# Six of the sequence DFT's passes, not five, as seven block products, with the sums of x and the weight chunks at earlier steps

## The chip, the cores and the metric

The kernel runs on one core of one Trainium2 chip. The metric is device time in microseconds (us) of one execution. The profile's names: PE is TensorE's matmul, PEld its weight load, DVE is VectorE, ACT is ScalarE, POOL is GpSimd, SP is SyncE, which here issues the transfers, and SPq is SP's queue.

## The reference, cut to what matters

One sublayer mixes along both axes by Fourier matrices, a second one is a gated feed-forward layer. x is 2048 x 448, the inner width is 1792, all in float32:

```
h  = x + Cr @ (ln(x) @ Dr.T) - Ci @ (ln(x) @ Di.T)     # Cr, Ci: 2048 x 2048
out = h + (gelu(ln(h) @ w_gate) * (ln(h) @ w_up)) @ w_down
```

The change lies in the first line: the products with the two 2048 x 2048 matrices. The kernel multiplies them with ln(x) first and applies the 448-wide matrices afterwards.

## The kernel before, in words

Every float32 operand is split in two halves of 16 bits, a high part (made on ACT) and the remainder (made on DVE), and each product is three matmuls: high by high, high by low, low by high.

The sequence DFT runs in `N_STEPS` = 64 steps (L405), written out in program order; nothing reorders them later. Steps 0 to 15 go over the 16 row tiles of x. From step 16 on, four steps make a pass, and each pass gives 256 rows of the result, for the real or the imaginary matrix. A step needs 128 x 1024 numbers of the matrix, called unit n: `seq_load` brings them in as `wr` (two transfers on SP, some steps ahead), `seq_hi` on ACT and `seq_lo` on DVE make the tile `ws`. Those two run three steps ahead of the matmuls that read the tile. There are 6 buffers of the tag `ws` and 5 of `wr`.

An ordinary step (L637) is 8 block products of three matmuls, 24 in all, each over 448 columns. A step from `FAST` on (L441) uses Strassen's scheme in one level: two groups of 7 block products over half the columns, that is 42 matmuls over 224 columns (`fast_mm`, L509). For this, DVE forms sums of blocks of the matrix (`fast_sums`, L460 to L462, tile `sums`), which ACT and DVE split (`fast_raw`, `fast_split`) into two `ws` tiles per unit, named `ws44_0` and `ws44_1` for unit 44. A unit is then made two steps ahead, except the first three, whose places are the list `fast_at` (L796). At the end of a fast pass `fast_out` puts the seven sums together on DVE (L538, tile `e`) and splits them into `zs`. After an ordinary pass ACT and DVE split the accumulators into `zs` directly (`z_out`).

The Strassen products also need sums of blocks of ln(x), the eight pieces t0 to t7: `t_load` brings rows of x in again, `t_norm` normalizes them on ACT, `t_sums` (DVE, L571 to L574) forms the sums, `t_hi` and `t_lo` split them. Step n of a pass reads pieces 2(n mod 4) and 2(n mod 4) + 1. A piece's steps stand in a table at L789.

Once two passes for the same rows are done, `z_turn` has SP transpose `zs` into `z` by four DMAs, and `hid_mm` (L719) applies the 448-wide matrix, 21 matmuls for each of two halves; these are put in at fixed steps: 36 and 37, 44 and 45, 52 and 53, 60 and 61 among others. Between all this the same engines prepare the feed-forward layer: 9 chunks of the gate and up weights (`Weights`, table `DFT_F` at L737) are loaded, summed on DVE in step n, split in steps n + 1 and n + 2, and stored to DRAM after step n + 3. Their raw tiles have two buffers, so a chunk's load waits until the chunk before the last has been split.

SP is one queue in program order: what stands behind a transfer that waits for DVE or PE waits too. The accumulators of the passes lie in a ring of seven PSUM banks; the seven banks are given names again for the feed-forward layer at L1289, where chunk 0 takes `a0`, `a1`, `a2` and chunk 1 takes `X`, `Y`, `Z`.

Of the kernel before, what the change touches and what calls it, by code (L numbers as in the profile page):

```python
# [32 lines left out]
def kernel(  # L33
# [172 lines left out]
    def down_load(n):  # L206
        place = (fpool, "dn_w", 3) if n > 1 else (fops, "xn" if n % 2 else "tt", 1)
        wd32[n] = place[0].tile([P, 4, HD], F32, tag=place[1], bufs=place[2], name=f"wd32_{n}")
        nc.sync.dma_start(wd32[n].rearrange("p (k c) d -> p k (c d)", k=2), w_down[n])
# [148 lines left out]
    def x_load(i):  # L358
        xt[i] = dft.tile([P, 1, D], F32, tag="xt", bufs=3, name=f"x{i}")
        nc.sync.dma_start(xt[i][:, 0, :], x[i * P : (i + 1) * P, :])  # L360
# [44 lines left out]
    N_STEPS = NT + 8 * (NP - 2)  # L405
# [7 lines left out]
    def seq_load(n):  # L413
        wr[n] = dft.tile([P, 8 * P], F32, tag="wr", bufs=5, name=f"wr{n}")
        if n < NT:
            nc.sync.dma_start(wr[n].rearrange("p (b t) -> p b t", b=4), w_seq[8 * (n % 2) + n // 2])
            return
        p, part, qq = step_of(n)
        for i in range(2):
            dst = wr[n][:, i * 4 * P : (i + 1) * 4 * P].rearrange("p (g t) -> p g t", g=2)  # L420
            nc.sync.dma_start(dst, w_seq[8 * p + 2 * qq + i][:, 2 * part : 2 * part + 2, :])
# [4 lines left out]
    def seq_hi(n):  # L426
        ws_tile(n)
        hi_part(ws[n][:, 0], wr[n], D_SC)

    def seq_lo(n):  # L430
        lo_part(ws[n][:, 1], wr[n], ws[n][:, 0], D_SC)
# [6 lines left out]

    FAST = N_STEPS - 20  # L441
    A_RAW = ("A12", "A11", "A22")
    FORMS = ("S3", "S1", "S2", "S4")
    T_OPS = ("T1", "T3", "T4", "T2")
# [22 lines left out]
    def fast_places(n):  # L467
        ring = dict(tag="ws", bufs=6)
        return (dict(tag="raw", bufs=2, pool=prep), ring) if n == FAST + 2 else (ring, ring)

# [27 lines left out]
    def fast_begin(n):  # L498
        fast_acc[n] = [ps_seq.tile([P, 512], F32, tag="mm", name=f"acc_f{n}_{k}") for k in range(4)]
# [59 lines left out]
    def t_load(j):  # L559
        tx[j] = [dft.tile([P, 1, D], F32, tag="xt", bufs=3, name=f"tx{j}_{k}")[:, 0, :] for k in range(2)]  # L560
        for k in range(2):
            i = 2 * j + 1 - k
            nc.sync.dma_start(tx[j][k], x[i * P : (i + 1) * P, :])

    def t_norm(j):
        for k in range(2):
            x_affine(tx[j][k], tx[j][k], 2 * j + 1 - k)

    def t_sums(j):
        (o1, o2), (e1, e2) = [(t[:, 0:HD], t[:, HD:D]) for t in tx[j]]  # L570
        V.tensor_sub(o1, o2, o1)  # L571
        V.tensor_sub(o2, e2, o2)
        V.tensor_sub(e2, e2, o1)
        V.tensor_sub(e1, e1, e2)  # L574
# [19 lines left out]
    def t_hi(j):  # L594
        fast_t[j] = t_tile(j)
        for dst, src in zip(t_views(j, 0), tx[j]):
            hi_part(dst, src)

    def t_lo(j):
        for dst, src, hi in zip(t_views(j, 1), tx[j], t_views(j, 0)):  # L600
            lo_part(dst, src, hi)
# [27 lines left out]
    def seq_acc(p, part, g, last=False):  # L629
        pool, tag = (ps_tr, "tr") if last else (ps_seq, "mm")  # L630
        acc[p, part, g] = pool.tile([P, 512], F32, tag=tag, name=f"acc{p}_{part}{g}")
# [102 lines left out]


    gu, gw = {}, {}
    DFT_F = ((13, 17), (11, 20), (9, 22), (7, 25), (5, 27), (3, 30), (0, 32), (1, 35), (2, 37))  # L737
    JIT_F = range(4, 13, 2)

    early, after = {}, {}  # L740

    def at(where, n, *what):
        where.setdefault(n, []).extend(what)
# [7 lines left out]
        nc.sync.dma_start(gw[f], w_dram[f])  # L751

    for i, (f, n) in enumerate(DFT_F):
        at(after, (n - 4, 0), lambda f=f, k=i % 2: gu.update({f: Weights(f, k)}))
        at(early, n, lambda f=f: gu[f].sums())
        at(early, n + 1, lambda f=f: gu[f].split(True))
        at(early, n + 2, lambda f=f: gu[f].split(False))
        at(after, (n + 3, 0), lambda f=f: gu[f].store())
# [6 lines left out]
    for p, (n, half) in enumerate(turns):  # L765
        b, j = divmod(p, 2)
# [19 lines left out]
    at(early, N_STEPS - 2, lambda: h_tile(NB - 1, 1))  # L786
    at(early, N_STEPS - 1, gelu_table)
    at(after, (N_STEPS - 2, 0), lambda: down_load(0), lambda: down_load(1))
    for j, n in ((0, 17), (1, 20), (4, 24), (5, 29), (6, 36), (2, 39), (3, 42), (7, 45)):  # L789
        at(after, (n - 2, 1), lambda j=j: t_load(j))  # L790
        at(early, n, lambda j=j: t_norm(j), lambda j=j: t_sums(j))
        at(after, (n, 0), lambda j=j: t_hi(j))
        at(after, (n, 1), lambda j=j: t_lo(j))


    fast_at = [FAST + n for n in (-4, -2, -1)] + list(range(FAST + 1, N_STEPS - 2))  # L796

# [34 lines left out]
    for n in range(N_STEPS):  # L832
        if n == 0:
            for key in first:
                seq_acc(*key, last=key == first[-1])
        elif n >= FAST and n % 4 == 0:
            fast_begin(n)
# [3 lines left out]
        if n + 3 < NT:  # L841
            x_load(n + 3)
        if n + 3 < FAST:
            seq_load(n + 5)

        if 0 < n < FAST - 3:
            seq_hi(n + 3)
# [6 lines left out]
        if n == 0:  # L854
            seq_lo(2)
        if n + 3 < FAST:
            seq_lo(n + 3)
# [406 lines left out]
    for q, t0, step, when in ((2, 6, 3, AT_A), (3, 14, 6, AT_B)):  # L1264
# [22 lines left out]
    right.close()  # L1287
    ps_ff = {
        tag: ctx.enter_context(tc.tile_pool(name=f"ps_{tag}", bufs=1, space=bass.MemoryType.PSUM, reuse_waits="tile"))  # L1289
        for tag in ("a0", "a1", "a3", "X", "Y", "Z", "a2")  # L1290
    }
    ps_ff["tr"] = ps_tr

# [11 lines left out]
    for t in range(NF):  # L1305
        w = gu.get(t + 2) if t + 2 in JIT_F else None
        n = PREP_AT.get(t)
# [90 lines left out]
    for t in range(NF, N_GU):  # L1398
        now, ahead = steps[t], steps.get(t + 1, [])
# [59 lines left out]
        for p, t0 in ended.items():  # L1459
            each = 3 if p < 3 else 2  # L1460
            n = each * (t - t0)
# [106 lines left out]
```

## Time and profile before

| | |
|---|---|
| median of 3 runs | 705.34 us (705.0 to 705.86) |
| the profiled execution, its own time | 706.23 us |
| its span, first to last instruction | 704.5 us |
| PE busy | 699.3 us |
| DVE busy | 536.5 us |
| ACT busy | 394.7 us |
| granted clock of TensorE | 1.0 throughout |

The span is 1.73 us shorter than the profiled execution's time, and that execution is 0.89 us above the median. In a row of a group, "x24" is the number of instructions, then come busy time and the mean of one; matmuls overlap each other, so their mean is longer than the distance between two. In the timeline and the chain of waits the first number is the start in us, the second the length. In the windows, each engine has its busy time in the stretch. In brackets stands the idle time ahead of a row and what ended it.

### The profile page before, as it was taken

Reading aid. Unit: us, or ns where it says so; the run is one execution under the profiler, and the core shown is the slowest. Engines: PE = TensorE matmul, PEld = TensorE weight load, DVE = VectorE, ACT = ScalarE, POOL = GpSimd, SP = SyncE. Lnnn points to the kernel's source line nnn. Section 1 sums busy time; section 2 is a strip of 40 time slices with the busy share of each in tenths; the row PEclk is TensorE's granted clock in tenths of the full one; section 3 lists DMA queues with packets and bytes.
Section 4 is the critical chain, followed back from the end, with each engine's and each line's share of the span. In section 5 each row is a group of like instructions: output and inputs, shape, how many; then the busy total and the mean of one; then the engine's idle time right before and its main releaser. Section 6 shows DMA issues by size and latency. Waiting matters only on the chain.

```text
span 704.5 us, 13462 instructions
## 1 busy us (share of the span) xinstructions
PE 699.3 (99%) x5092; PEld 494.0 (70%) x5092; DVE 536.5 (76%) x1164; ACT 394.7 (56%) x778; POOL 97.3 (14%) x88
## 2 busy tenths in 40 slices
PE   9999999999999999999999999999999999999998
PEld 5555555555555689897644444469999999999997
DVE  6988646685958779797547788667677876899786
ACT  5876546675565755564526566545555453555531
POOL 0000000000000000000223333312020111232324
PEclk9999999999999999999999999999999999999999
DMA  8788768999999457366845877797888985888612
GB/s 270 242 246 275 178 210 192 321 295 254 298 298 320 125 136 198 117 164 218 218 156 202 283 254 195 201 313 246 235 238 303 268 283 175 286 287 299 228 50 79
DMA packets 116321, 161.29 MB, mean 229 GB/s; under 512 B 61984, under 2 KB 80544, under 8 KB 116256
## 3 DMA queue, kind: packets, MB, share of 16 engines
q1 hardware_dynamic: 116256, 160.43, 74.8%
q8 instruction: 40, 0.66, 0.4%
q14 instruction: 25, 0.20, 0.1%
HBM read 112.16 MB, written 34.34 MB: 208 GB/s over the span
## 4 chain that ended last, share of the span: by engine, by line
PE 96%; DMA 1%; DVE 1%; issue 1%; SPq 1%; ACT 0%; POOL 0%; POOLq 0%; DVEq 0%
PE acc L637 28%; PE acc_d L1228 15%; PE pY L1024 14%; PE acc_f L509 11%; PE y L719 9%; PE pX L1024 9%; PE pZ L1024 9%; DMA hid_dram<-hs 1%; PE pw L102 1%; SPq L1141 0%; DVE wd L114 0%; SPq L294 0%; DVE xs L112 0%; ACT dn_w L108 0%; ACT v L954 0%
## 5 line engine op out<-in xcount | busy, mean ns | idle before, releaser
L637 PE MATMUL acc<-xs,ws 128*128 128x448 f16 x1056 | 201.3, 352 | 0.0
L1024 PEld LDWEIGHTS <-gw 128*128 128x128 f16 x1443 | 140.8, 98 | 51.9 <-DMA gw<-w_dram 0.2
L637 PEld LDWEIGHTS <-ws 128*128 128x128 f16 x1056 | 103.2, 98 | 96.6 <-ACT ws L108 0.3
L1228 PE MATMUL acc_d<-wd,dn_w 128*128 128x224 f16 x1008 | 110.9, 259 | 0.5 <-DVE dn_w L112 0.5
L1228 PEld LDWEIGHTS <-dn_w 128*128 128x128 f16 x1008 | 96.8, 98 | 2.8 <-DVE dn_w L112 0.9
L1024 PE MATMUL pY<-hops,gw 128*128 128x256 f16 (+1 forms) x629 | 98.1, 298 | 0.0
L1118 POOL TENSOR_TENSOR hs<-hs,c 128x256 f32<-128x256 f32 (+1 forms) x42 | 62.1, 1478 | 246.7 <-ACT c L1116 168.9
L114 DVE SCALAR_TENSOR_TENSOR ws<-wr,ws 128x1024 f16<-128x1024 f32 (+2 forms) x66 | 73.1, 1109 | 26.7 <-ACT ws L108 25.3
L509 PEld LDWEIGHTS <-ws 128*128 128x128 f16 x840 | 80.5, 98 | 1.3
L108 ACT ACTIVATE ws<-wr 128x1024 f16<-128x1024 f32 (+2 forms) x66 | 62.7, 954 | 11.0 <-DMA wr<-in_w_seq_dram 9.9
L1024 PE MATMUL pX<-hops,gw 128*128 128x256 f16 (+1 forms) x407 | 67.1, 298 | 0.0
L1024 PE MATMUL pZ<-hops,gw 128*128 128x256 f16 (+1 forms) x407 | 67.1, 298 | 0.0
L719 PE MATMUL y<-wh,z 128*128 128x448 f16 x336 | 66.2, 352 | 0.0
L509 PE MATMUL acc_f<-t,ws 128*128 128x224 f16 x480 | 56.9, 259 | 0.0
L215 POOL TENSOR_TENSOR wd_s<-wd 128x448 f32<-128x448 f32 x7 | 9.4, 1349 | 339.4 <-DMA wd<-in_w_down_dram 338.6
L1069 ACT ACTIVATE pY<-pX 128x256 f32<-128x256 f32 (+1 forms) x42 | 18.4, 439 | 66.3 <-PE pX L1024 65.8
L719 PEld LDWEIGHTS <-z 128*128 128x128 f16 x336 | 32.9, 98 | 29.7
L1034 DVE SCALAR_TENSOR_TENSOR c<-pZ,u 128x256 f32<-128x256 f32 (+1 forms) x42 | 21.4, 511 | 38.1 <-PE pZ L1024 22.4
L1080 ACT ACTIVATE u<-pY 128x256 f32<-128x256 f32 (+1 forms) x42 | 19.1, 454 | 54.0 <-PE pY L1024 53.9
L509 PE MATMUL acc_f<-xs,ws 128*128 128x224 f16 x360 | 45.6, 259 | 0.0
L112 DVE TENSOR_TENSOR dn_w<-dn_s,dn_w 128x640 f16<-128x640 f32 x48 | 42.3, 881 | 1.4 <-ACT dn_w L108 1.4
L108 ACT ACTIVATE dn_w<-dn_s 128x640 f16<-128x640 f32 x48 | 34.9, 727 | 12.5 <-DVE dn_s L1190 12.4
(144 smaller groups left out, 887.0 us busy)
## 6 DMA issues: line engine op xcount, KB each, us to landing
gw<-w_dram SPq DMA_DIRECT2D x37, 896.0 KB, 6.4
wr<-in_w_seq_dram SPq DMA_DIRECT2D x100, 256.0 KB, 4.6
hid_dram<-hs SPq DMA_DIRECT2D x27, 512.0 KB, 5.8
hid<-hid_dram SPq DMA_DIRECT2D x54, 256.0 KB, 5.5
w_dram<-gu_w SPq DMA_DIRECT2D x14, 896.0 KB, 6.4
gu_raw<-in_w_gu_dram SPq DMA_DIRECT2D x28, 384.0 KB, 5.9
wr<-in_w_seq_dram SPq DMA_DIRECT2D x14, 512.0 KB, 5.7
x<-in_x_dram SPq DMA_DIRECT2D x16, 224.0 KB, 2.9
```

The costliest lines, as they stand in the source:

```text
L108: A.activation(dst, src, AF.Copy, scale=scale)
L112: V.tensor_sub(dst, src, hi)
L114: V.scalar_tensor_tensor(dst, src, scale, hi, op0=ALU.mult, op1=ALU.subtract)
L509: PE.matmul(fast_sum(n, k), fast_a(n, i, lw, a), fast_b(j, lx, b), start=j == 0 and m == 0 and k % 2 == 0, stop=j == NT // 2 - 1 and m == ...
L637: PE.matmul(acc[key][:, :D], w[:, lw, block * P : (block + 1) * P], xs[c][:, lx, :], start=c == 0 and m == 0, stop=c == NT - 1 and m == 2,)
L719: PE.matmul(y[:, :D], z[p][:, lz, k, g * P : (g + 1) * P], wh[:, lw, k, :], start=p == NP - 1 and k == 0 and m == 0, stop=k == 6 and m == ...
L1024: PE.matmul(ps, w[:, wl, wa + ws, :], ops[:, m + ms, :], start=first and n == 0, stop=last and n == len(terms) - 1, skip_group_check=True,)
L1034: V.scalar_tensor_tensor(dst, ps, SC, other, op0=ALU.mult, op1=ALU.add)
L1069: A.activation(self.Y, self.X, AF.Copy)
L1080: A.activation(self.u2, self.Y, AF.Copy, scale=SC)
L1118: G.tensor_mul(c22, c22, self.cols(self.c12))
L1228: PE.matmul(ps, w[:, la, a, :], wd[n][:, lb, b, :], start=n == 0 and m == 0 and opens, stop=n == NC - 1 and m == 2, skip_group_check=True,)
```

## The change

Three tables and one rule are edited, and one list of bank names:

```diff
-    FAST = N_STEPS - 20
+    FAST = N_STEPS - 24
...
-    DFT_F = ((13, 17), (11, 20), (9, 22), (7, 25), (5, 27), (3, 30), (0, 32), (1, 35), (2, 37))
+    DFT_F = ((13, 16), (11, 18), (9, 20), (7, 22), (5, 25), (3, 27), (0, 29), (1, 31), (2, 34))
...
     for i, (f, n) in enumerate(DFT_F):
-        at(after, (n - 4, 0), lambda f=f, k=i % 2: gu.update({f: Weights(f, k)}))
+        ahead = 4 if i < 2 or n - DFT_F[i - 2][1] > 4 else 3
+        at(after, (n - ahead, 0), lambda f=f, k=i % 2: gu.update({f: Weights(f, k)}))
...
-    for j, n in ((0, 17), (1, 20), (4, 24), (5, 29), (6, 36), (2, 39), (3, 42), (7, 45)):
+    for j, n in ((0, 17), (1, 20), (4, 24), (5, 28), (6, 31), (2, 35), (3, 38), (7, 41)):
...
-        for tag in ("a0", "a1", "a3", "X", "Y", "Z", "a2")
+        for tag in ("a3", "X", "Y", "Z", "a0", "a1", "a2")
```

`FAST` goes from 44 to 40, so steps 40 to 43 become a fast pass, and the three units that are made early move from steps 40, 42, 43 to 36, 38, 39. The pieces t5, t6, t2, t3 and t7 move by one to five steps, the weight chunks by one to four.

On PE, at the border of steps 39 and 40 (acc4 is the pass of steps 36 to 39, acc5 and acc_f40 the next one), there stands before:

```order
L637 LDWEIGHTS ws39_2124
L637 MATMUL acc4_11_2120<-xs15_887,ws39_2124 128x448
L637 LDWEIGHTS ws40_2197
L637 MATMUL acc5_00_2355<-xs0_202,ws40_2197 128x448
L637 LDWEIGHTS ws40_2197
L637 MATMUL acc5_00_2355<-xs0_202,ws40_2197 128x448
```

That is an ordinary step, 24 matmuls over 448 columns. On PE at the same border there stands now:

```order
L637 LDWEIGHTS ws39_2170
L637 MATMUL acc4_11_2166<-xs15_890,ws39_2170 128x448
L509 LDWEIGHTS ws40_0_2174
L509 MATMUL acc_f40_0_2398<-xs1_223,ws40_0_2174 128x224
L509 LDWEIGHTS ws40_0_2174
L509 MATMUL acc_f40_0_2398<-xs1_223,ws40_0_2174 128x224
```

The matmuls of step 40 are half as wide, and over four steps there are 168 of them where 96 stood.

On DVE, in steps 40 to 42 (sums and ws are unit 43 and 44, tx7 and t7 the last piece of x), there stands now between the drain of the pass before (zs4) and unit 44:

```order
L114 SCALAR_TENSOR_TENSOR zs4_2141<-acc4_11_2166,zs4_2141 128x448
L460 TENSOR_TENSOR sums43_2451<-wr43_2306 128x512
L461 TENSOR_TENSOR sums43_2451<-sums43_2451,wr43_2306 128x256
L462 TENSOR_TENSOR sums43_2451<-wr43_2306,sums43_2451 128x256
L114 SCALAR_TENSOR_TENSOR ws43_0_2452<-wr43_2306,ws43_0_2452 128x768
L114 SCALAR_TENSOR_TENSOR ws43_1_2453<-sums43_2451,ws43_1_2453 128x1024
L571 TENSOR_TENSOR tx7_0_2394<-tx7_0_2394 128x224
L572 TENSOR_TENSOR tx7_0_2394<-tx7_1_2395,tx7_0_2394 128x224
L573 TENSOR_TENSOR tx7_1_2395<-tx7_1_2395,tx7_0_2394 128x224
L574 TENSOR_TENSOR tx7_1_2395<-tx7_1_2395 128x224
L112 TENSOR_TENSOR t7_2492<-tx7_0_2394,t7_2492 128x448
L112 TENSOR_TENSOR t7_2492<-tx7_1_2395,t7_2492 128x448
```

Before, this stretch held the units 44 and 45 ahead of the first fast pass, then the piece t3; now a fast pass is under way while DVE makes unit 43, t7 and unit 44.

On SP, ahead of the transposes of zs3 that `hid_mm` of step 36 reads, there stands before:

```order
L421 DMA wr36_1874<-in_w_seq_dram 128x512 x2
L312 DMA gu_raw1_1911<-in_w_gu_dram 128x768 x2
L733 DMA h_dram2_139<-hx1_0_1521 128x896
L421 DMA wr37_1931<-in_w_seq_dram 128x512 x2
L693 DMA hx1_1_1953<-in_x_dram 128x2x448
L658 DMA_TRANSPOSE z3_1967<-zs3_1666 128x7x128 x4
```

The weight tile of chunk 1 comes in just ahead of zs3 there. On SP at the same place there stands now:

```order
L421 DMA wr36_1904<-in_w_seq_dram 128x512 x2
L733 DMA h_dram2_139<-hx1_0_1539 128x896
L421 DMA wr37_1973<-in_w_seq_dram 128x512 x2
L693 DMA hx1_1_1991<-in_x_dram 128x2x448
L351 DMA w_dram0_145<-gu_w0_1845 128x3584
L658 DMA_TRANSPOSE z3_2006<-zs3_1688 128x7x128 x4
```

The load of chunk 1 has moved further ahead and the store of chunk 0 has come in front of the transposes. Counted from the transposes of zs2 to those of zs3, SP issues one store and one pair of x tiles (t6) more than before.

## The prediction

> **What bounds the kernel now.** The page first: which engine fills the span, and at which clock.
>
> ```profile
> PE 699.3 (99%) x5092; PEld 494.0 (70%) x5092; DVE 536.5 (76%) x1164; ACT 394.7 (56%) x778; POOL 97.3 (14%) x88
> PEclk9999999999999999999999999999999999999999
> ```
>
> PE is busy for all but 5.2 us of the 704.5 us span. A busy PE need not be at its best, so the second view is what PE waits for, over the whole span:
>
> ```profile
> PE pw L102 <- POOL sign_t L93: 1.4, 1, 1.4
> PE acc_d L1228 <- DVE dn_w L112: 0.5, 1, 0.5
> PE acc_d L1228 <- ACT v L954: 0.2, 1, 0.2
> ```
>
> One wait at the start, two near the end, none in the sequence DFT. What remains is how fast the matmuls follow each other; the chain of waits merges them into pieces, so a piece's length by its count is the distance from one to the next:
>
> ```profile
> 107.49 18.16 PE acc L637 x96
> 196.01 3.97 PE y L719 x21
> 208.50 29.51 PE acc L637 x156
> 251.99 28.17 PE acc_f L509 x294
> ```
>
> 18.16 by 96 and 29.51 by 156 are 189.2 ns for a matmul over 448 columns, 28.17 by 294 is 95.8 ns for one over 224. So a step costs PE 24 x 189.2 = 4.54 us as an ordinary one and 42 x 95.8 = 4.02 us as a fast one. The windows of passes confirm it: the ordinary passes of steps 32 to 35, 36 to 39 (with two `hid_mm`) and 40 to 43, and the fast pass of 48 to 51, which has none.
>
> ```profile
> 175.42:193.58 18.16, 18.16 (x97) 9.39 (x96) 15.91 (x32) 10.97 (x19) 0.00 (x0) 1.00 1.05 296
> 193.58:219.69 26.11, 26.11 (x140) 13.51 (x139) 17.80 (x35) 17.06 (x34) 0.00 (x0) 1.00 1.06 318
> 219.69:237.85 18.16, 18.16 (x98) 9.39 (x97) 13.21 (x22) 10.43 (x16) 0.00 (x0) 1.00 0.80 219
> ...
> 261.89:277.99 16.10, 16.10 (x170) 16.10 (x169) 15.74 (x27) 8.65 (x15) 0.00 (x0) 1.00 0.78 200
> ```
>
> The stretch is PE alone, each pass 100% busy. A saving of PE time there reaches the end in full, unless an operand becomes late. After PE and PEld a row has DVE: in a fast pass without `hid_mm` it works 15.74 of 16.10 us. That is the resource to watch.
>
> **The change part by part.** *PE.* Steps 40 to 43 turn from 96 matmuls of 189.2 ns into 168 of 95.8 ns: 18.16 - 16.10 = 2.06 us less. The `hid_mm` blocks stay at their steps. This is the whole gain.
>
> The row that could speak against it is that of the weight loads, since a fast step has 42 of them for 24:
>
> ```profile
> L509 PEld LDWEIGHTS <-ws 128*128 128x128 f16 x840 | 80.5, 98 | 1.3
> ```
>
> A load lasts 98 ns, hardly longer than the 95.8 ns between matmuls; were it the pace, a step would cost 42 x 98 = 4.12 us and the gain 4 x (4.54 - 4.12) = 1.7 us. The chain's 95.8 ns already holds in the five passes that exist, so I take 2.06. The Trainium skill, page "TensorE: Matmul & The Clock Gate", section "Back-to-back issue gap", speaks against such a change: it says that in a sustained stream of load and matmul pairs 128 columns take about 81 ns and 512 about 131 ns, so that half the width saves little of the time. Interpolated from that page, an estimate, 224 columns take 93.5 ns and 448 take 122.7, a fast step is 0.98 us slower than an ordinary one, and the sum would be +3.9 us in place of -2.06. The trace disagrees with it for the wide ones, 189.2 ns.
>
> *DVE, steps 40 to 43.* The work of a unit is read from the timeline of DVE at the tightest place, units 50 and 51, with the matmul that reads unit 50's second tile:
>
> ```profile
> 266.07 0.63 DVE L114 SCALAR_TENSOR_TENSOR zs<-e,zs 128x448 f16<-128x448 f32 x1
> 266.62 0.68 DVE L460 TENSOR_TENSOR sums<-wr 128x512 f32<-128x512 f32 x1
> ...
> 268.14 0.95 DVE L114 SCALAR_TENSOR_TENSOR ws<-wr,ws 128x768 f16<-128x768 f32 x1
> 269.01 1.22 DVE L114 SCALAR_TENSOR_TENSOR ws<-sums,ws 128x1024 f16<-128x1024 f32 x1
> 270.14 0.68 DVE L460 TENSOR_TENSOR sums<-wr 128x512 f32<-128x512 f32 x1
> ...
> 270.52 0.74 PE L509 MATMUL acc_f<-t,ws 128*128 128x224 f16 x6
> ```
>
> A unit costs DVE 270.14 - 266.62 = 3.52 us, and its last tile was ready 0.3 us ahead of PE (270.23 against 270.52): so thin is the cover of the fast passes today. A piece of x and the drain of an ordinary pass cost, from the timeline around the start of step 40 at 219.69:
>
> ```profile
> 216.39 0.38 DVE L571 TENSOR_TENSOR tx<-tx 128x224 f32<-128x224 f32 x1
> 217.73 0.39 DVE L574 TENSOR_TENSOR tx<-tx 128x224 f32<-128x224 f32 x1
> ...
> 220.46 0.62 DVE L114 SCALAR_TENSOR_TENSOR zs<-acc,zs 128x448 f16<-128x448 f32 x1 [1.65 <-ACT zs L108]
> 221.00 1.15 DVE L112 TENSOR_TENSOR t<-tx,t 128x448 f16<-128x448 f32 x2
> ```
>
> The four sums take 1.7 us, the remainders 1.15, the drain is over 1.4 us into the pass. Now count from the start of step 40: drain 1.4; unit 43's sums and first tile to 3.8; its second tile takes a buffer that PE frees at the end of step 40 (4.02), so with about 1.2 on ACT and 1.2 on DVE it ends at 6.4; t7's sums 1.7, about 0.5 for ACT's half, remainders 1.15: 9.8; unit 44: 13.3. PE wants unit 43 at 12.1, t7 at about 13.5, unit 44 at 16.1: margins 5.7, 3.7 and 2.8 us. Behind it stand unit 45, the norm of the last early tile of h (moved out of an ordinary pass into this one) and `fast_out`, with two `hid_mm` (7.94 us) as cover in steps 44 and 45, the relief that pass 44 to 47 has now. Since t7 and t3 have left pass 44 to 47, DVE should come to unit 50 earlier than today. I cost DVE at nothing; without that cover each us costs one.
>
> *DVE and SP, steps 16 to 39.* Chunks and pieces come at up to five steps sooner. A chunk costs DVE (sums, two splits):
>
> ```profile
> 206.79 0.56 DVE L317 TENSOR_TENSOR gu_s<-gu_raw 128x384 f32<-128x384 f32 x1
> 208.19 0.42 DVE L320 TENSOR_TENSOR gu_s<-gu_raw,gu_s 128x256 f32<-128x256 f32 x1
> ...
> 212.34 1.02 DVE L114 SCALAR_TENSOR_TENSOR gu_w<-gu_raw,gu_w 128x512 f16<-128x512 f32 x2
> ...
> 215.19 1.29 DVE L114 SCALAR_TENSOR_TENSOR gu_w<-gu_s,gu_w 128x512 f16<-128x512 f32 x2
> ```
>
> 1.82 + 1.02 + 1.29 = 4.1 us. Pass by pass, by the tables: steps 32 to 35 lose 7.2 us of chunk work (chunks 3, 0, 1) and gain 5.1 (chunks 1, 2) and t2 (2.9), so 15.9 becomes about 16.7 of 18.16. Steps 36 to 39 lose 5.1 of chunk work, three `seq_lo` (1.2 each, as the 128x1024 row above), t6 and t2 (5.8) and gain three units (10.6) and t3 (2.9): 17.8 becomes about 16.8 of 26.11. DVE still fits into every pass. Steps 28 to 31 gain the most, chunk 0 and chunk 1's sums for those and one split of chunk 3 (3.1 us) and t6 (2.9), in a pass with two `hid_mm` in which DVE now waits 4.01 us at one place alone (below). The place that worries me is z3, which `hid_mm` reads at 196.01. DVE and SP there:
>
> ```profile
> 171.47 1.22 DVE L114 SCALAR_TENSOR_TENSOR ws<-wr,ws 128x1024 f16<-128x1024 f32 x1 [4.01 <-ACT ws L108]
> ...
> 176.41 1.16 DVE L114 SCALAR_TENSOR_TENSOR zs<-acc,zs 128x448 f16<-128x448 f32 x2 [1.91 <-ACT zs L108]
> ...
> 169.71 1.05 SPq L421 DMA_DIRECT2D wr<-in_w_seq_dram  x2
> 173.66 0.80 SPq L312 DMA_DIRECT2D gu_raw<-in_w_gu_dram  x2
> 176.99 8.35 SPq L658 DMA_TRANSPOSE z<-zs  x4
> 185.40 1.04 SPq L421 DMA_DIRECT2D wr<-in_w_seq_dram  x2
> ```
>
> zs3's drain ended at 177.6 and the last transpose was issued by 185.3. In front of the drain now stand a chunk's sums and t6's sums (1.82 + 1.7): it ends some 3.7 us later. In the queue there are one store (896 KB) and 448 KB of x more, 1344 KB at the 296 to 318 GB/s of the windows about 4.4 us, against 2.9 us in which SP stood idle (170.76 to 173.66). Both delays overlap. With these rows for a transfer's landing,
>
> ```profile
> w_dram<-gu_w SPq DMA_DIRECT2D x9, 896.0 KB, 7.3
> z<-zs SPq DMA_TRANSPOSE x18, 3.9
> ```
>
> z3 landed by 185.3 + 3.9 = 189.2 at the latest, 6.8 us ahead; about 4.4 less leaves some 2.4 us. No cost, then, with thin cover. `wr` loads behind it are delayed alike, but their units are wanted three steps later.
>
> *Bank names.* Two banks fewer are taken before the first fast pass and four more later, so the ring stops at another place; the renamed list again gives chunk 0 the three banks that the last pass does not hold. Were it not so, PE would wait for the last drain, in the rows
>
> ```profile
> 341.81 1.41 DVE L538 SCALAR_TENSOR_TENSOR e<-acc_f,e 128x224 f32<-128x224 f32 x4 [0.33 <-PE acc_f L509]
> 342.38 1.29 PE pX L1024 x6
> ```
>
> 343.22 - 342.38 = 0.84 us. I take 0. All later work is in the same order and shifts as a whole.
>
> Sum: -2.06 us. For the profiled execution that is 704.5 - 2.06 = 702.4 us of span and 704.2 us of time; that execution lay 0.89 us above the median, so the median goes from 705.34 to **703.3 us**. What a measurement can tell from no change is 0.2%, 1.41 us: the borders are 703.93 and 706.75.
>
> **The rivals.** *Part of the gain is lost to an operand* (unit 43 to 45, or z3): a stall of 0.65 to 3.47 us puts it within 0.2%; with 2 us, 705.3. For it: the 0.3 us margin at unit 50 and margins of 2.4 to 2.8 us by a count of single rows. Against it: every operand counted above comes out with a margin, and PE waits nowhere there now. 0.12.
>
> *Slower: z3 late.* One mechanism: SP stands behind chunk 2's raw load, which waits for DVE's split of chunk 0, and behind DVE's drain, so that z3 lands over 6.8 + 3.5 = 10.3 us later than now; PE would stand at step 36. Two more waits of DVE for ACT like the 4.01 us one and the 4.4 us of transfers, if nothing overlapped, make 12.4: a stall of 5.6, 708.9 us. 0.07.
>
> *A price per matmul, not per column.* If the narrow matmuls cost as much as the 110 ns that 110.9 us by 1008 gives for another group of the same width,
>
> ```profile
> L1228 PE MATMUL acc_d<-wd,dn_w 128*128 128x224 f16 x1008 | 110.9, 259 | 0.5 <-DVE dn_w L112 0.5
> ```
>
> a fast step takes 4.62 us and the change +0.3: 705.7. The page of the Trainium skill above points this way. Against it stands 95.8 ns in 294 matmuls of the same form. 0.02.
>
> **How the numbers follow.** Forecast 0.79, rivals 0.12, 0.07 and 0.02. The forecast's own spread is the three runs' 0.4 us, the 1.7 us of the weight loads and a stall under 0.65 on the one side, and the 0.7 us of late PE waits that might vanish on the other: 702.5 to 703.9. To hold 8 in 10 the range takes a little of the first rival: 702.5 to 704.6. Faster by over 0.2%: 0.79; within: 0.12 + 0.02 = 0.14; slower: 0.07.
>
> **What would show it.** Right: steps 40 to 43 in a window of 16.1 us with PE busy throughout, 1008 matmuls of acc_f at 95.8 ns, no new row among PE's waits, unit 50 ready over 1 us ahead. Wrong: a PE wait on `ws` from DVE after step 40, on z from DMA at step 36, or a chain that leaves PE between 170 and 260 us.

## The result, and the profile after

| | before | after |
|---|---|---|
| median | 705.93 us (705.0 to 706.54, 6 runs) | 711.79 us (710.67 to 712.91, 6 runs) |
| profiled execution, its span | 706.23, 704.5 us | 712.12, 710.0 us |

The ratio is 1.0082 (95% interval 1.0072 to 1.0092): 5.9 us slower, where 703.3 us (702.5 to 704.6) was forecast.

The page of the changed kernel, busy times, and below it what PE waits for:

```profile
PE 698.4 (98%) x5164; PEld 500.3 (70%) x5164; DVE 550.6 (78%) x1187; ACT 399.3 (56%) x787; POOL 95.2 (13%) x88
```

```profile
PE y L719 <- ACT y L700: 5.5, 2, 4.1
PE pw L102 <- POOL sign_t L93: 1.4, 1, 1.4
PE acc_d L1229 <- DVE dn_w L112: 1.0, 2, 0.7
...
```

The first row is new. PE waits twice, 5.5 us in all, for an instruction of ACT at L700, and no wait for `ws` or for z has come. L700 is `hid_seed`. The sums `y` of both halves of `hid_mm` use the same PSUM bank (tag `tr`, one buffer). When PE has finished the first half, ACT reads it out (`hid_out`, L708 to L710) and then writes h of the second half into the bank, on top of which `hid_mm` adds. That hand-over has the time of one step. The timeline of PE at step 37, and that of ACT from just after step 36 has begun:

```profile
195.48 4.14 PE L719 MATMUL y<-wh,z 128*128 128x448 f16 x21
199.46 4.70 PE L637 MATMUL acc<-xs,ws 128*128 128x448 f16 x24
208.28 5.82 PE L719 MATMUL y<-wh,z 128*128 128x448 f16 x21 [4.12 <-ACT y L700]
```

```profile
198.58 1.04 ACT L108 ACTIVATE t<-tx 128x448 f16<-128x448 f32 x2 [2.98 <-DMA w_dram<-gu_w]
199.53 0.52 ACT L108 ACTIVATE zs<-acc 128x448 f16<-128x448 f32 x1
199.95 1.04 ACT L108 ACTIVATE ws<-wr 128x1024 f16<-128x1024 f32 x1
202.40 0.84 ACT L108 ACTIVATE ws<-wr 128x768 f16<-128x768 f32 x1 [1.40 <-DMA wr<-in_w_seq_dram]
203.55 0.63 ACT L108 ACTIVATE ws<-sums 128x512 f16<-128x512 f32 x1 [0.31 <-DVE sums L460]
204.47 0.63 ACT L108 ACTIVATE ws<-sums 128x512 f16<-128x512 f32 x1 [0.29 <-DVE sums L462]
205.01 1.13 ACT L108 ACTIVATE gu_w<-gu_s 128x512 f16<-128x512 f32 x2
206.05 0.52 ACT L708 ACTIVATE hx<-y 128x448 f32<-128x448 f32 x1
...
207.68 0.55 ACT L700 ACTIVATE y<-hx 128x448 f32<-128x448 f32 x1
```

PE has the first half ready at 199.6. ACT reads it at 206.05: ahead of it in its queue stand t2, unit 39, unit 40 (the 128x768 and the two 128x512 rows of `sums`) and chunk 2's second split. In before, the same two instructions come 5.8 us sooner, and the unit 40 of that kernel stands behind them (the 128x1024 row):

```profile
200.20 0.52 ACT L708 ACTIVATE hx<-y 128x448 f32<-128x448 f32 x1
...
201.84 0.55 ACT L700 ACTIVATE y<-hx 128x448 f32<-128x448 f32 x1
...
203.26 1.04 ACT L108 ACTIVATE ws<-wr 128x1024 f16<-128x1024 f32 x1
```

The data of unit 40, `wr40`, land at 202.78 before and at 202.38 after, so that transfer is no later. What has changed is the order: as the first unit of a fast pass it is prepared in step 36, one step sooner, and so ahead of the hand-over.

Behind the wait the second half takes 5.82 us where the first took 4.14. The windows (time of the stretch, PE, PEld, DVE, ACT, POOL, then the granted clock, the DMA share and GB/s) over the start and the middle of that half:

```profile
208.28:209.30 1.02, 1.02 (x5) 0.48 (x5) 0.85 (x2) 0.00 (x0) 0.00 (x0) 0.92 0.91 369
209.30:212.29 2.99, 2.99 (x10) 1.22 (x9) 0.00 (x0) 0.00 (x0) 0.00 (x0) 0.50 1.01 314
```

The clock goes to 0.50 a microsecond after PE has resumed, for 3 us. Last, the windows of steps 32 to 35, 36 to 39, the new fast pass, and the fast pass of steps 48 to 51:

```profile
175.06:193.21 18.15, 18.15 (x97) 9.39 (x96) 14.91 (x38) 13.03 (x22) 0.00 (x0) 1.00 1.10 289
193.21:225.29 32.08, 27.96 (x140) 13.97 (x139) 21.99 (x43) 18.32 (x37) 0.00 (x0) 0.95 0.79 233
225.29:241.39 16.10, 16.10 (x170) 16.10 (x169) 14.58 (x30) 10.02 (x17) 0.00 (x0) 1.00 0.63 156
266.93:283.03 16.10, 16.10 (x170) 16.10 (x169) 15.74 (x27) 9.37 (x16) 0.00 (x0) 1.00 0.93 216
```

The new fast pass takes the 16.10 us that were forecast. The pass of steps 36 to 39 takes 32.08 us in place of 26.11, 5.97 more: 4.12 for the wait and 1.85 behind it (1.68 for the longer half; the rest because the row counts the wait from the end of the last matmul, and matmuls overlap). The span adds up: -2.06 for that pass, +4.12 and +1.34 for the two waits (5.5 together), +1.85 for the slow matmuls, +0.56 for the waits for `dn_w` (1.02 after, 0.46 before), and -0.37 because this execution got through its first steps sooner: +5.44 of the 5.5 measured. The profiled executions themselves are 5.89 us apart. The other 0.39 lies outside the span: the time exceeds it by 2.12 to 2.21 us in the six runs after, by 1.73 to 1.90 in those of before, for a reason that no run shows.

### The profile page after: what moved, and what is told of

Same layout as the page of the kernel before. It is cut to its first block, busy times and chain, and to the rows that moved or that the text cites. A ratio compares the mean times of both kernels' runs of the same rounds, so it can differ in the third digit from the quotient of the medians.

```text
span 710.0 us, 13654 instructions
## 1 busy us (share of the span) xinstructions
PE 698.4 (98%) x5164; PEld 500.3 (70%) x5164; DVE 550.6 (78%) x1187; ACT 399.3 (56%) x787; POOL 95.2 (13%) x88
## 4 chain that ended last, share of the span: by engine, by line
PE 88%; DVE 5%; ACT 3%; DMA 3%; issue 2%; SPq 0%; DVEq 0%; ACTq 0%
PE acc L637 21%; PE acc_d L1229 15%; PE pY L1025 14%; PE acc_f L509 11%; PE pZ L1025 9%; PE pX L1025 9%; PE y L719 8%; DMA hid_dram<-hs 1%; DMA w_dram<-gu_w 1%; DVE ws L114 1%; ACT ws L108 0%; DVE sums L460 0%; DMA x<-in_x_dram 0%; ACT xs L108 0%; DVE gu_w L114 0%
## 5 line engine op out<-in xcount | busy, mean ns | idle before, releaser
L637 PE MATMUL acc<-xs,ws 128*128 128x448 f16 x960 | 183.2, 352 | 0.4 <-DVE xs L149 0.4
L637 PEld LDWEIGHTS <-ws 128*128 128x128 f16 x960 | 93.8, 98 | 88.2 <-issue 0.6
L509 PEld LDWEIGHTS <-ws 128*128 128x128 f16 x1008 | 96.6, 98 | 1.3
L1119 POOL TENSOR_TENSOR hs<-hs,c 128x256 f32<-128x256 f32 (+1 forms) x42 | 59.7, 1421 | 249.1 <-ACT c L1117 189.2
L719 PE MATMUL y<-wh,z 128*128 128x448 f16 x336 | 67.8, 359 | 5.5 <-ACT y L700 5.5
L509 PE MATMUL acc_f<-t,ws 128*128 128x224 f16 x576 | 68.3, 259 | 0.0
L509 PE MATMUL acc_f<-xs,ws 128*128 128x224 f16 x432 | 54.8, 259 | 0.0
```

Source lines behind the costliest of these rows:

```text
L509: PE.matmul(fast_sum(n, k), fast_a(n, i, lw, a), fast_b(j, lx, b), start=j == 0 and m == 0 and k % 2 == 0, stop=j == NT // 2 - 1 and m == ...
L637: PE.matmul(acc[key][:, :D], w[:, lw, block * P : (block + 1) * P], xs[c][:, lx, :], start=c == 0 and m == 0, stop=c == NT - 1 and m == 2,)
L719: PE.matmul(y[:, :D], z[p][:, lz, k, g * P : (g + 1) * P], wh[:, lw, k, :], start=p == NP - 1 and k == 0 and m == 0, stop=k == 6 and m == ...
L1119: G.tensor_mul(c22, c22, self.cols(self.c12))
```

## The experiments

Theory H: the hand-over of y on ACT is late, since unit 40 is now ahead of it, and all else is as forecast. Rival O: the preparation moved ahead is too much for DVE and SP, and the wait at step 37 is only where that shows. Rival S: ACT is late because t2's high part stood 2.98 us until chunk 1's store had read the tile that t2 goes into. All kernels below are the changed kernel with one edit, if nothing else is said. The 705.66 to 705.91 us of before are its medians beside them.

**Give the hand-over another step.** One place for the second half, and its two followers along with it:

```diff
+        late = int(p in (3, 4))
-            at(after, (m + g, int(p >= 5 and g)), lambda p=p, g=g: hid_mm(p, g), lambda p=p, g=g: hid_out(p, g))
+            at(after, (m + g + (late and g), int(p >= 5 and g)), lambda p=p, g=g: hid_mm(p, g), lambda p=p, g=g: hid_out(p, g))
...
-        at(early, m + 2 if p < 5 else N_STEPS - 7 + p, lambda b=b, j=j: ffn_rstd(b, j))
-        at(after, (m + 2, 0), lambda b=b, j=j: h_store(b, j))
+        at(early, m + 2 + late if p < 5 else N_STEPS - 7 + p, lambda b=b, j=j: ffn_rstd(b, j))
+        at(after, (m + 2 + late, 0), lambda b=b, j=j: h_store(b, j))
```

> The changed kernel with the second half of hid_mm of passes 3 and 4 put one step later (after the first half of steps 38 and 46 in place of 37 and 45; the rstd and the store of h that follow go one step later with it). Nothing of the preparation is moved. Theory H (the hand-over of the one bank of y through ScalarE is late, and nothing else): PE would get to hid_mm(3,1) at 204.16 + 4.54 = 208.70 us, after the seed that ended at 208.23, so the waits of 4.12 and 1.34 us and the 1.85 us of matmuls at half speed behind the first go: 711.8 - 7.3 = 704.5 us, within 703.7 to 704.9; no row 'PE y <- ACT y' over 0.3 us. Rival O (the preparation moved ahead doesn't fit on VectorE and SyncE in steps 28 to 39): the stall only turns up at another wait of PE, and the time stays at 708 to 712 us.

Measured: 704.92 us, at the upper edge of what H gave; before 705.91, ratio 0.9987 (0.9978 to 0.9995). What PE waits for, pieces of the chain of waits, and the window of the new fast pass:

```profile
PE pw L102 <- POOL sign_t L93: 1.4, 1, 1.4
PE acc_d L1230 <- DVE dn_w L112: 1.0, 2, 0.7
PE acc_d L1230 <- ACT v L956: 0.2, 1, 0.2
```

```profile
125.96 3.97 PE y L719 x21
...
220.17 18.11 PE acc_f L509 x189
...
340.63 1.29 PE pX L1026 x6
```

```profile
220.00:236.10 16.10, 16.10 (x169) 16.09 (x168) 14.71 (x35) 10.02 (x17) 0.00 (x0) 1.00 0.68 157
```

Both waits for y are gone and no other has taken their place in the sequence DFT. From the first of these pieces to the start of gate and up there are 214.67 us; in the chain of before the same two pieces start at 125.64 and 342.38, 216.74 apart: 2.07 us less, the forecast's 2.06. Rival O is out: all the early preparation still stands in this kernel, and PE doesn't wait for it. The medians show only 0.99 of it. Of the missing 1.07 us, some 0.6 goes to the waits for `dn_w`, 1.05 us in place of 0.46 (more on that below), and about 0.2 lies outside the span, by which the time is longer than it by 1.87 to 2.12 us here; the last 0.3 is not traced.

With pass 3 alone one step later (`late = int(p in (3,))`):

> The changed kernel with the second half of hid_mm of pass 3 alone one step later; that of pass 4 stays at step 45. Theory H: no wait at step 37; at step 45 the seed of hid_mm(4,1) ends some 1.4 us after PE gets there (247.56 against 250.14 - 4.02 = 246.12 in the kernel that moves both), too short a wait for slow matmuls behind it: 704.9 + 1.4 = 706.3 us. If the second wait was only an echo of the first: 704.9.

Measured: 706.48 us, before 705.76. What PE waits for y:

```profile
PE y L719 <- ACT y L700: 1.3, 1, 1.3
```

The second wait is one of its own, as forecast. By the timeline of ACT it follows the new fast pass: ahead of `hid_out(4,0)` stand the `zs` halves of that pass, which wait 2.90 us for DVE's sums `e`, then unit 46 and a split of h for the feed-forward layer; before the change step 44 had no fast pass behind it. That cause is read from the trace (2.90 us in this kernel too) and was not tried by itself.

Half a step later for pass 3, `int(p in (3, 5, 6) and g)` in the place above:

> The changed kernel with hid_mm(3,1) half a step later (after the second half of step 37). Theory H: PE gets there at 204.16 + 2.27 = 206.43, the seed comes at 208.23, so the wait is 1.8 us in place of 4.12; the wait of 1.34 at step 45 stays. If the half speed of the matmuls behind the wait hangs on the wait's length, as none follow the 1.34 us wait, they go as well: 711.8 - 2.3 - 1.85 = 707.7 us. If they come after a wait of 1.8 us too: 709.5. Rival O: 711 to 712 us, with the wait elsewhere.

Measured: 709.74 us, before 705.91. The timeline of PE at both waits (the second row ends with its window, after 16 of the 21 matmuls), and windows over the matmuls behind them:

```profile
208.43 4.13 PE L719 MATMUL y<-wh,z 128*128 128x448 f16 x21 [2.02 <-ACT y L700]
...
250.33 4.87 PE L719 MATMUL y<-wh,z 128*128 128x448 f16 x16 [2.58 <-ACT y L700]
```

```profile
208.43:212.50 4.07, 4.07 (x22) 2.15 (x22) 0.85 (x2) 0.00 (x0) 0.00 (x0) 1.00 1.00 333
250.33:254.50 4.17, 4.17 (x14) 1.77 (x14) 4.06 (x7) 1.76 (x3) 0.00 (x0) 0.59 0.91 197
```

The first wait is 2.0 for the 1.8 expected, and full clock behind it. The second grew from 1.34 to 2.58, which I had not expected, and has the slow matmuls behind it. Both of my figures for the time (707.7, 709.5) left that out, so that the second being near is chance. The profiled execution is also the longest of the six (711.37 us); the two shortest, 708.02 and 708.53, have a mean clock of 0.999 and 1.0 in place of its 0.997, too high for matmuls at half speed as long as these.

**Change what stands ahead of the hand-over.** Unit 40 behind it, on ACT and DVE alike and together with the load of unit 42 that follows it, everything else in its place:

```diff
+    def first_unit():
+        fast_sums(FAST)
+        fast_raw(FAST)
+        fast_split(FAST)
+        seq_load(FAST + 2)
+    at(after, (FAST - 4, 0), first_unit)
...
-        if n in fast_at:
+        if n in fast_at and n > FAST - 4:
```

> The changed kernel with unit 40, the first of the new fast pass, prepared half a step later: in the order of ScalarE and VectorE behind hid_out(3,0) and the seed of hid_mm(3,1) in place of ahead of them. All else is as in the changed kernel, hid_mm(3,1) and hid_mm(4,1) too. Theory H: ScalarE is through ws39 at 201.0 us and through chunk 2's split at 202.05, hid_out(3,0) and the seed end at 204.2: the wait at step 37 falls from 4.12 to 0 to 0.3 us, the slow matmuls behind it go; the second wait, at step 45, stays at 1.3 to 2.6 us. 705.3 to 707.3 us. Rival O (VectorE or SyncE have too much to do): the wait at step 37 stays over 2 us or comes back at ws40, 709 us and more.

Measured: 706.27 us, before 705.76. What PE waits for y, and the hand-over on ACT:

```profile
PE y L719 <- ACT y L700: 1.3, 1, 1.3
```

```profile
200.99 0.53 ACT L708 ACTIVATE hx<-y 128x448 f32<-128x448 f32 x1
...
202.63 0.55 ACT L700 ACTIVATE y<-hx 128x448 f32<-128x448 f32 x1
203.12 0.83 ACT L108 ACTIVATE ws<-wr 128x768 f16<-128x768 f32 x1
```

The order of this one unit takes the whole wait at step 37 away, 4.12 us and the slow matmuls. The hand-over is now 5 us sooner, and unit 40 follows it.

Only chunk 2's second split behind it (its call goes from `early[36]` to the list after the first half of step 36):

> The changed kernel with the second split of chunk 2 (two high parts on ScalarE, 1.04 us from start to start) behind hid_out(3,0) and the seed in place of ahead of them; unit 40 stays ahead. Theory H, with the wait set by what ScalarE does between wr40's landing and hid_out: the wait at step 37 falls by those 1.04 us, from 4.12 to 3.1, the wait at step 45 stays: 710.7 us with the slow matmuls, 708.9 without. If ScalarE's own work were no part of the wait (only wr40's landing and VectorE's sums): 711.8.

Measured: 710.64 us, before 705.76. The timeline of PE at step 37 (17 of the 21 matmuls):

```profile
207.30 4.93 PE L719 MATMUL y<-wh,z 128*128 128x448 f16 x17 [2.95 <-ACT y L700]
```

2.95 us for the 3.1 expected: ACT's own time ahead of the hand-over counts in full (1.17 us less wait for 1.04 us of work). The slow matmuls stayed after a wait of 2.95.

Piece t2 one step later, `(2, 36)` for `(2, 35)`:

> The changed kernel with the piece t2 one step later (step 36 in place of 35), so that its high part on ScalarE, which waited 2.98 us for chunk 1's store to have read the tile that it goes into, stands behind hid_out(3,0) and the seed. Rival S (this wait for the store is what makes the hand-over late): the wait before hid_mm(3,1) shrinks by about 3 us and the half speed behind it goes, 711.8 - 3.0 - 1.85 = 707.0 us. Theory H in the form that unit 40 sets the time: ScalarE then waits for wr40's landing at 202.4 us instead, hid_out stays at about 206 and the time at 711 to 712.3 us.

Measured: 714.3 us, before 705.91. ACT:

```profile
203.49 0.84 ACT L108 ACTIVATE ws<-wr 128x768 f16<-128x768 f32 x1 [6.56 <-DMA wr<-in_w_seq_dram]
...
206.71 1.40 ACT L382 ACTIVATE tx<-tx,affine 128x448 f32<-128x448 f32 x2
208.01 0.52 ACT L708 ACTIVATE hx<-y 128x448 f32<-128x448 f32 x1
...
209.65 0.55 ACT L700 ACTIVATE y<-hx 128x448 f32<-128x448 f32 x1
```

Rival S is out. The wait for the store is gone, and ACT stands 6.56 us for `wr40` instead. That the time got worse by 2.5 us, which neither theory gave, comes from what I had overlooked: t2's normalizing (1.40 us, L382) moved along and landed ahead of the hand-over, and `wr40` came 1.1 us later.

The two tables alone, with their rule for the loads, `FAST = N_STEPS - 20` and the old bank names:

> The two tables of the change (chunks and pieces of x sooner) alone: five fast passes and the list of banks as before. Theory H: what stood in front of hid_out(3,0) on ScalarE was unit 40, about 4.1 us with its waits for wr40 and for its sums; it is now behind, so the wait before hid_mm(3,1) is 0 to 0.5 us and the time that of before, 705.7 to 706.6 us. Rival O: the tables alone overload VectorE and SyncE: the wait of 3 to 4 us at step 37 stays, 709 to 712 us.

Measured: 705.77 us, before 705.91, ratio 0.9998 (0.9989 to 1.0006). ACT at the hand-over:

```profile
201.28 0.53 ACT L708 ACTIVATE hx<-y 128x448 f32<-128x448 f32 x1
...
202.92 0.55 ACT L700 ACTIVATE y<-hx 128x448 f32<-128x448 f32 x1
203.41 1.04 ACT L108 ACTIVATE ws<-wr 128x1024 f16<-128x1024 f32 x1
```

PE has no wait for y here: the tables cost nothing by themselves, though they use up 1.2 us of the hand-over's slack (L700 at 202.92, 201.84 before, with PE 0.16 us sooner here). Counted from the start of PE's first half, ACT begins the hand-over after 4.35 us before, 5.59 with the tables alone and 10.57 in the changed kernel. So the sixth fast pass, with unit 40 in front, takes 5.0 us more.

**The two fixes together by the other way.** Unit 40 behind the hand-over, and `late = int(p in (4,))`:

> The changed kernel with unit 40 behind hid_out(3,0) and the seed, and with the second half of hid_mm of pass 4 one step later; that of pass 3 stays at step 37. Theory H: both waits for y go, by another way than moving hid_mm(3,1): 2.06 us less than before, less the 0.6 us more of waits for dn_w: 704.3 to 705.1 us, like the kernel that moves both second halves (704.9). Rival O: 706 us or more.

Measured: 704.83 us, before 705.66, ratio 0.9989 (0.9980 to 0.9998), the same as the kernel that moves both second halves, and PE has no wait for y. At step 45 the two kernels have the same edit. At step 37 their edits have only the hand-over in common, and both take the wait away.

**Bank names.** The kernel with both second halves later and the old list of names:

> The kernel with the second halves of passes 3 and 4 one step later (704.9 us), with the list of PSUM bank names as it was before the change. If the renaming is needed, PE waits for the last drain before the first matmul of gate and up, some 0.84 us: 705.8. If it makes no difference: 704.9. If the new wait of 0.71 us for dn_w at 473.5 us comes from the names: 704.3.

Measured: 705.89 us, before 705.76. What PE waits for:

```profile
PE pX L1026 <- DVE e L538: 0.9, 1, 0.9
PE acc_d L1230 <- DVE dn_w L112: 0.7, 1, 0.7
```

The renaming is worth 0.9 us, and the wait of 0.7 us for `dn_w` stands under either list.

**The wait for dn_w.** The new one is the longer of the two, 0.7 us. On DVE, one drain of gate and up stands ahead of `dn_w`. It writes the tile hs_14, of which there are two. The rows of before, of the kernel with both second halves later, and of that kernel with three tiles:

```diff
-                hs[self.t] = fpool.tile([P, 8, P], F32, tag="hs", bufs=2, ...)
+                hs[self.t] = fpool.tile([P, 8, P], F32, tag="hs", bufs=3, ...)
...
-        hid_in[d] = fpool.tile([P, 4, P], F32, tag="hid", bufs=6, ...)
+        hid_in[d] = fpool.tile([P, 4, P], F32, tag="hid", bufs=4, ...)
```

> The kernel with both second halves one step later (704.9 us), with three tiles of hs in place of two, paid for with four tiles of hid in place of six. The new wait of 0.71 us for dn_w at 473.5 us goes back to VectorE, which stands before hs_14 from 471.9 to 473.4. If it stands there for the store of hs_12 (issued 464.70, landed 473.31), whose tile hs_14 takes, that wait goes and PE waits 0.2 us at most at this place: 704.9 - 0.5 to 0.7 = 704.3 us, unless the fewer tiles of hid make a new wait. If VectorE waits for PE, as the page names it, nothing changes: 704.9.

```profile
474.49 0.42 DVE L1034 SCALAR_TENSOR_TENSOR hs<-pY,m 128x256 f32<-128x256 f32 x1 [0.73 <-DMA hid_dram<-hs]
```

```profile
473.43 0.42 DVE L1036 SCALAR_TENSOR_TENSOR hs<-pY,m 128x256 f32<-128x256 f32 x1 [1.54 <-PE pX L1026]
```

```profile
470.87 0.42 DVE L1036 SCALAR_TENSOR_TENSOR hs<-pY,m 128x256 f32<-128x256 f32 x1
```

With three tiles DVE doesn't wait, and the waits for `dn_w` are gone from the list. In the second row's kernel the store of hs_12, issued at 464.70, landed at 473.31, 0.12 us ahead of the row. So it was that store, and the releaser "PE pX" of the second row is a wrong guess of the view. But the time is 708.34 us, before 705.66, because the fewer tiles of hid make a new wait, the one for which the expectation left a door open and no size:

```profile
PE pX L1026 <- DMA gw<-w_dram: 5.7, 5, 1.9
```

The store takes 8.02 us from issue to landing before, 8.61 in the kernel with both second halves later, 8.55 in the changed one, with the same transfers around it. It takes 8.0 with the tables alone and 8.5 to 8.6 in every profiled kernel with six fast passes, so it goes with the sixth pass. Why it is 0.6 us slower there stays open.

## Why the prediction was wrong, step by step

- **PE, -2.06 us: right.** The new fast pass takes 16.10 us, and up to gate and up the kernel without waits for y gains 2.07.
- **Weight loads: right.** 18.11 us for 189 matmuls is 95.8 ns each. The sustained figures of the Trainium skill's section "Back-to-back issue gap" (page "TensorE: Matmul & The Clock Gate"), which by the prediction's interpolation, an estimate, would have made this pass slower, don't hold in this kernel.
- **DVE in steps 40 to 43: right.** Counted from the start of step 40 (220.00), unit 43, t7 and unit 44 were to be done after 6.4, 9.8 and 13.3 us. The rows of the kernel with both second halves later:

```profile
225.12 1.23 DVE L114 SCALAR_TENSOR_TENSOR ws<-sums,ws 128x1024 f16<-128x1024 f32 x1 [0.74 <-ACT ws L108]
...
228.70 0.62 DVE L112 TENSOR_TENSOR t<-tx,t 128x448 f16<-128x448 f32 x1 [0.17 <-ACT t L108]
...
231.63 1.22 DVE L114 SCALAR_TENSOR_TENSOR ws<-sums,ws 128x1024 f16<-128x1024 f32 x1
```

  That is 6.35, 9.32 and 12.85. Unit 50 was to be over 1 us ahead: it is ready at 267.5 and read at 268.8.
- **DVE and SP in steps 16 to 39, "no cost": the step that failed.** What it looked at came out well: z3 landed at 189.2, 6.3 us ahead of PE, where I had feared 2.4. (It had landed at 187.4 before, not 189.2, so it came 1.8 us later where I had allowed 4.4; and the sums put in front of its drain, 1.82 + 1.7, make 3.5 and not 3.7.) DVE was mis-sized (14.9 and 22.0 us in the two passes, forecast 16.7 and 16.8), but it fits: 21.8 of 26.1 us where PE does not wait. What it didn't look at was ACT. The only deadlines it set were those of z3, of the units and of the pieces. The sentence "The `hid_mm` blocks stay at their steps" was taken to mean that they cost nothing; but between the two halves of each there is a hand-over on ACT, and of unit 40, which the change moves one step ahead, only DVE's part was counted. The page showed ACT 56% busy, and I took an engine with free time for one that can't be late. Its slack could have been read in the trace of before: the seed ended at 201.84 + 0.55 = 202.4, and PE came there at 196.01 + 3.97 + 4.54 = 204.5, 2.1 us later; unit 40 with its waits keeps ACT from 200.99 to 205.01, 4.0 us. The whole sum: 1.2 us for the tables and 5.0 for the sixth pass (unit 40's 4.0 and 1.0 of smaller delays, most of it ahead of unit 40), less 2.1 of slack, is the wait of 4.1.
- **Bank names, 0, and 0.84 if not: right.** 0.9 measured for the old list.
- **"All later work shifts as a whole": wrong by 0.6 us**, at the store of hs_12.
- **The rival on the other side** had the right sign, the wrong place (z3) and too small a price, since it had no second wait and no slow clock: 708.9 against 711.8.
- **What would show it wrong** held in its last item: the chain left PE between 170 and 260 us, at ACT. Three of its four signs of being right held as well (the 16.10 us window, 1008 matmuls at 95.8 ns, unit 50 over 1 us ahead); only the list of PE's waits told of the hand-over.

## What to carry to other kernels

Before moving work ahead in time, list for every in-order engine what the work is put in front of, and for each bank or tile with a single buffer the hand-over between its two users; the slack is the time from the releasing instruction's end to PE's arrival, and an engine at 56% can still be 4 us late at one point. When an otherwise idle engine delays the bound one, first try the order (one unit behind the hand-over, or the consumer one step later): here that turned 5.9 us of loss into 0.8 to 1.0 us of gain, without taking anything out.

## What the runs showed of the hardware

A wait of PE can cost more than its length. In the profiled executions the clock stayed at 1.00 after waits of 1.34 and 2.02 us; after 2.58, 2.95, 4.12 and 5.62 us it was 0.50 for about 3 to 5 us, beginning at once (2.95, 5.62) or within a microsecond of PE's return. In the kernel with t2 later, after 5.62 us:

```profile
210.60:215.00 4.40, 4.40 (x13) 1.74 (x12) 2.61 (x5) 0.56 (x2) 0.00 (x0) 0.50 0.61 207
```

The Trainium skill, page "TensorE: Matmul & The Clock Gate", section "HAM oscillation — how this bites in real kernels", asks for no idle gap of PE over some 3.4 us. Here 2.58 us was enough to lose the full clock in one execution, 2.02 was not in another. The length of the wait alone does not settle it: 3.3 us at half clock take 0.002 off the mean clock of a run, and of the changed kernel's six runs five have a mean of 0.997 or 0.998 but one, of 710.70 us, has 1.0. What decides is not shown.
